# Batch 0 in whole products, batch 1's scores by subtiles, half of batch 2's second layer by seven products, and a new order

## The chip, the cores and the metric

The kernel runs on one core of a Trainium2 chip. Its engines are TensorE (PE in the rows; PEld its weight loads), VectorE (DVE), ScalarE (ACT), GpSimd (POOL) and SyncE (SP), which issues all transfers. The time is the device time of one execution, in microseconds, as the median of several runs. Each kernel also has one profiled execution, from which all rows are taken.

## What is computed

Local attention with block summaries, then a mixing of tokens of rank 32, then two dense layers over the channels, for 4 batches of 768 tokens, 8 heads of 64 channels and 512 channels in all:

```python
def _attn_ref(q, k, v):                      # (4, 8, 768, 64) each
    k_sum = k.reshape(B, H, nb, 32, D).max(axis=3)
    v_sum = v.reshape(B, H, nb, 32, D).mean(axis=3)
    scores = concat(where(|i - j| < 16, q @ k.T / 8, -1e9), q @ k_sum.T / 8 + log(32))
    return softmax(scores) @ concat(v, v_sum)

def _moe_ref(x, U, V, w_ch1, w_ch2):         # x: (4, 768, 512)
    h = x.transpose(0, 2, 1) @ U @ V         # over the tokens, rank 32
    u = x + h.transpose(0, 2, 1)
    return u + maximum(u @ w_ch1, 0) @ w_ch2 # 512 -> 2048 -> 512
```

U, V, w_ch1 and w_ch2 come as float64 and are turned into float32 on the chip.

## The kernel before

**Precision and products.** A dense product takes three products of a high and a low part each (high x high, high x low, low x high), every one a matrix product of TensorE in fp32r. A "part" is made by ScalarE, which rounds (`nc.scalar.copy(hi, ...)`), and by GpSimd or VectorE, which subtracts (`lo = whole - hi`). In the rows, `L1320` is the up layer (512 to 2048) of batches 1 to 3, `L1416` their down layer (2048 to 512), `L1522` batch 3's down layer, `L1024` and `L1049` are up and down of batch 0.

**Four batches, one after the other.** TensorE works on the dense layers of batch b, while the attention of batch b+1 is strewn in between: scores (`S`), exponentials (`E`, on VectorE and ScalarE), turning of the probabilities by VectorE and a way through HBM (`T`, `s`, `f`), values (`P`), normalising (`N`), the mixing (`M`, `J`, `O`). The attention of batch 0 has nothing beside it and fills the first 50 us.

**Batch 0** (L1300 on): for each of 16 slices f of the hidden layer and each half hf of the tokens (384), `up_channel` (L1015) makes 12 products of 384 columns over the four channel tiles, `up_out` takes the positive part as gates, and `down_rows` (L1043) takes three token tiles of the gates as the standing operand against 512 columns of w_ch2, 9 products. Its output has tokens on the rows. `leave_row` copies it out of PSUM, and `finish_rows` (L1063) turns it by 24 transposes (`ps_o`, L1068) within batch 1's up phase, adds u and stores it. Weights come by `load_weight` (L804) into five places for each layer, are turned to float32 (`t`), split, and, for the later batches, stored in HBM together with sums of them (`U`, `Us`, `D`).

**Batches 1 to 3, up** (`up_phase`, L1333): the matrices are cut in quarters, and seven products take the place of eight; a step is 6 products of 384 columns. **Down** (`down_phase`, L1396) in batches 1 and 2: whole products, channels on the rows; for each f four tiles of 512 columns and two of 2 x 256, 24 products, kept in six PSUM banks over all f. Batch 3 (`second_phase`, L1502) uses seven products for the down layer too: 56 steps of 6 products of 384 columns. Its operands are sums and differences of hidden quarters, made by `second_operand` (L1433) into places that `st.ring` hands out.

**Batch 1's scores** (`scores`, L436): a tile of 128 queries against 120 keys, with 128 rows of which half are zeros by `clear_gaps`, three tiles in a bank. Batches 0, 2 and 3 use `scores_by_subtiles` (L454): products of 64 x 64 in four corners of the array, 12 for a head, in two banks.

**Order.** `PLAN` is a text of words, cut by slashes. Each word writes one operation; at each step of TensorE's dense work `go()` (L1292) writes the words up to the next slash. A word with a dot ahead belongs to batch 0's attention. `F` loads a weight of a later batch, `p0` makes its high part and `p1` its low part. Each engine does its operations in the order in which they were written and waits only for data and places. `keep_busy` (L1147, `ps_w`) writes filler products that nothing reads.

```python
for f in range(NF):
    for hf in range(2):
        g = first.pop() if first else up_out(up(st, hf, f))
        go()
        if prev is not None:
            ...
            down_rows(accs[phf], pf, pg, pf == 0, pf == NF - 1)
            go()
        prev = (f, hf, g)
```

## Time and profile before

| | |
|---|---|
| median of 3 runs (lowest, highest) | 624.52 us (622.56, 624.90) |
| profiled execution | 623.3 us |
| its span in the trace | 621.5 us |
| TensorE, VectorE, ScalarE, GpSimd busy | 97%, 69%, 56%, 47% of the span |
| moved by transfers | 148.29 MB, 239 GB/s over the span |

The trace has a start and a duration for each operation. Neighbouring matrix products overlap in it, so that the duration of one (some 340 ns for 384 columns) is longer than its distance to the next. The chain of waits goes back from the last operation to what released it; in it, a piece's length is the time until the next piece. A matrix product on fp32 data has two records.

### The profile page before, as it was taken

The numbers are of one execution on the slowest core, as the hardware profiler recorded it, in microseconds if no ns is written. First come the engines' busy times: TensorE is split into PE (matmuls) and PEld (weight loads), VectorE is DVE, ScalarE is ACT, GpSimd is POOL, SyncE is SP. The second block draws the span as 40 slices with busy tenths as digits, with TensorE's granted clock in tenths as the row PEclk, the third lists the DMA queues.
The fourth block names the chain that finished last, engine by engine and source line by source line (L and its number), as shares of the span: only waits on it lengthen the run. The fifth ranks groups of instructions, "written<-read, shape, count | busy, mean of one in ns | idle before, by whom it ended". The sixth has DMA issues, their size and how long they took to land.

```text
span 621.5 us, 14548 instructions
## 1 busy us (share of the span) xinstructions
PE 605.7 (97%) x5336; PEld 550.0 (88%) x5336; DVE 427.1 (69%) x1141; ACT 349.6 (56%) x796; POOL 292.2 (47%) x360
## 2 busy tenths in 40 slices
PE   4899999999999999999999999999999999999997
PEld 2678989889888999998888899998888899999997
DVE  3778576767866877888788754665555652678994
ACT  1867575654563567665544556765452646675720
POOL 4451342534245868765443788663232676640000
PEclk9999999999999999999999999999999999999999
DMA  7997999999788788788889678778989653446443
GB/s 220 264 278 265 290 296 291 300 301 304 260 242 239 244 281 275 238 254 263 253 264 294 200 259 223 194 227 220 306 247 308 203 197 118 125 144 248 147 148 113
DMA packets 97702, 148.29 MB, mean 239 GB/s; under 512 B 9696, under 2 KB 68064, under 8 KB 97632
## 3 DMA queue, kind: packets, MB, share of 16 engines
q1 hardware_dynamic: 97632, 147.38, 77.2%
q8 instruction: 42, 0.69, 0.5%
q14 instruction: 28, 0.23, 0.1%
HBM read 104.67 MB, written 42.66 MB: 237 GB/s over the span
## 4 chain that ended last, share of the span: by engine, by line
PE 89%; DMA 5%; SPq 2%; ACT 1%; DVE 1%; issue 1%; POOL 0%; DVEq 0%
PE ps_h L1320 28%; PE acc L1416 19%; PE ps_h L1024 10%; PE acc L1049 10%; PE accx L1522 4%; PE ps_x L607 3%; PE accy L1522 3%; PE accz L1522 3%; PE ps_s L468 2%; PE ps_s L445 2%; DMA place<-rows 1%; DMA rows<-place 1%; DMA place<-in_v 1%; DMA place<-in_k 1%; PE ps_m L637 1%; PE ps_x L593 1%
## 5 line engine op out<-in xcount | busy, mean ns | idle before, releaser
L971 POOL TENSOR_TENSOR parts<-whole,parts 128x512 fp32r<-128x512 f32 (+1 forms) x128 | 160.5, 1269 | 96.8 <-ACT parts L967 84.3
L1320 PE MATMUL ps_h<-place,parts 128*128 128x384 f32 x1008 | 180.4, 336 | 0.0
L1320 PEld LDWEIGHTS ps_h<-place,parts 128*128 128x128 f32 x1008 | 174.4, 188 | 1.5 <-issue 0.5
L1416 PE MATMUL acc<-gh,parts 128*128 128x256 f32 (+1 forms) x512 | 134.2, 342 | 0.0
L1416 PEld LDWEIGHTS acc<-gh,parts 128*128 128x128 f32 x512 | 88.4, 189 | 12.1 <-issue 1.2
L967 ACT CAST parts<-whole 128x512 fp32r<-128x512 f32 (+1 forms) x144 | 80.1, 581 | 12.9 <-DMA whole<-down 4.0
L1416 PE MATMUL acc<-gl,parts 128*128 128x512 f32 (+1 forms) x256 | 86.5, 338 | 0.0
L278 POOL TENSOR_TENSOR place<-val,place 128x512 fp32r<-128x512 f32 x29 | 38.1, 1328 | 95.5 <-ACT place L277 63.0
L1024 PE MATMUL ps_h<-place 128*128 128x384 f32 x384 | 73.8, 340 | 0.5 <-DVE gl L1040 0.5
L1024 PEld LDWEIGHTS ps_h<-place 128*128 128x128 f32 x384 | 67.0, 188 | 3.2 <-DVE gl L1040 0.9
L503 ACT ACTIVATE e<-e,neg 128x120 f32<-128x120 f32 x144 | 51.6, 390 | 31.3 <-DVE neg L493 30.3
L1049 PE MATMUL acc<-place,gh 128*128 128x512 f32 x192 | 66.5, 400 | 0.0
L1389 ACT ACTIVATE gh<-place 128x768 fp32r<-128x768 f32 x32 | 26.9, 844 | 51.5 <-PE acc L1416 51.4
L1394 DVE SCALAR_TENSOR_TENSOR gl<-place,gh 128x768 fp32r<-128x768 f32 x32 | 36.1, 1129 | 25.4 <-ACT gh L1389 25.1
L1416 PEld LDWEIGHTS acc<-gl,parts 128*128 128x128 f32 x256 | 48.5, 189 | 4.3
L1049 PEld LDWEIGHTS acc<-place,gh 128*128 128x128 f32 x192 | 36.0, 188 | 7.6 <-ACT gh L1039 0.2
L747 POOL TENSOR_TENSOR place<-tmp,place 128x384 fp32r<-128x384 f32 x24 | 26.8, 1126 | 29.8 <-ACT place L743 29.8
L1039 ACT ACTIVATE gh<-ps_h 128x384 fp32r<-128x384 f32 x32 | 15.7, 490 | 43.5 <-PE ps_h L1024 43.4
L1040 DVE SCALAR_TENSOR_TENSOR gl<-ps_h,gh 128x384 fp32r<-128x384 f32 x32 | 17.8, 555 | 32.1 <-ACT gh L1039 32.1
L493 DVE CUSTOM_DVE_ANT_0 e<-ps_s,mask_sb 128x120 f32<-128x120 f32 x144 | 34.8, 275 | 6.0 <-PE ps_s L445 3.3
L1049 PE MATMUL acc<-place,gl 128*128 128x512 f32 x96 | 37.7, 393 | 0.0
L523 DVE STREAM_TRANSPOSE squares<-e 128x768 f32<-128x768 f32 x24 | 23.3, 971 | 16.6 <-ACT e L503 14.6
(152 smaller groups left out, 985.2 us busy)
## 6 DMA issues: line engine op xcount, KB each, us to landing
place<-in_w SPq DMA_DIRECT2D x32, 512.0 KB, 5.9
whole<-up SPq DMA_DIRECT2D x24, 512.0 KB, 4.9
there<-squares SPq DMA_DIRECT2D x24, 384.0 KB, 4.7
at<-there SPq DMA_DIRECT2D x96, 96.0 KB, 3.9
whole<-up SPq DMA_DIRECT2D x24, 384.0 KB, 4.5
whole<-down SPq DMA_DIRECT2D x16, 512.0 KB, 5.9
vt<-in_v SPq DMA_DIRECT2D x48, 146.2 KB, 4.4
kt<-in_k SPq DMA_DIRECT2D x24, 288.0 KB, 5.0
```

The lines of the kernel that those rows point to most:

```text
L278: engine.tensor_tensor(lo, val, f32(hi), ALU.subtract)
L493: nc.vector.tensor_tensor_reduce(out=e[:, u, :], in0=ps[:, i * KC : (i + 1) * KC], in1=mask_sb[:, m, :], scale=-SCALE, scalar=BIG, op0=ALU ...
L503: nc.scalar.activation(e[:, u, :], e[:, u, :], AF.Exp, bias=st.neg[h][:, u : u + 1], scale=-1.0,)
L967: nc.scalar.copy(hi, whole)
L971: (nc.vector if key[0] == "second" else nc.gpsimd).tensor_tensor(lo, whole, f32(hi), ALU.subtract)
L1024: nc.tensor.matmul(ps[:, :NH], w_split[0, f][:, c % 2, part_w, c // 2], ut[c], start=(c == 0 and n == 0), stop=(c == NC - 1 and n == 2),)
L1049: nc.tensor.matmul(acc[t], gt[:, sl], w_split[1, f][:, part_w], start=(first and j == 0), stop=(last and j == 2),)
L1320: nc.tensor.matmul(ps, a[:, sa, i], b[i][:, sb], start=(first and n == 0), stop=(n == 5), skip_group_check=not first,)
L1389: nc.scalar.activation(gh, h, AF.Relu)
L1394: nc.vector.scalar_tensor_tensor(gl, h, 0.0, f32(gh), ALU.max, ALU.subtract)
L1416: nc.tensor.matmul(place, w[:, part_w, c * P : (c + 1) * P], gt[:, q0:q1], start=(f == 0 and i == 0 and j == 0), stop=(f == NF - 1 and j = ...
L1522: nc.tensor.matmul(ps[:, part], w[j][:, sa, c * P : (c + 1) * P], gate[sb][:, part], start=fresh and q == 0 and j == 0 and k == 0, stop=(q ...
```

## The change

- **Batch 0, up:** no longer by `up_channel` and gates at once. `first_up_phase` keeps the 12 products of 384 columns per slice and half, in two half groups of 6 (channels 0 and 2, then 1 and 3); the first four groups do their first halves ahead, so that up can begin while channels 1 and 3 are still being mixed. The result goes to the hidden places, and gates come later, as in batches 1 and 2. The heads are taken in the order 0, 1, 4, 5, 2, 3, 6, 7.
- **Batch 0, down:** by channels, in the `down_phase` of batches 1 and 2; `leave_row`, `finish_rows` and its transposes go, and each output tile leaves at the end of its sum.
- **Batch 1's scores:** by `scores_by_subtiles`; `scores` and `clear_gaps` go.
- **Batch 2's down:** the first four of eight pairs of slices by seven products (28 steps of 6), the other four by whole products as before.
- **Weights of batch 0** come through the same three places as the later batches' (`load_place`), and are split by the same `p` words; a third word, `p2`, makes a low part on VectorE. Sums of weights may be made on GpSimd (`wp`).
- **PLAN** is written anew: 557 steps, 481 before, with 13 fillers ahead of the first up product, 6 before. Steps and order of batch 3's two phases stay.

```diff
-SEVEN = (3,)
+SEVEN = {2: 4, 3: 8}
+AHEAD = 4
+HEADS = (0, 1, 4, 5, 2, 3, 6, 7)
...
-    def weight_place(i, f, dt=F32):
-        return wt.tile([P, 2 * DM], dt, name="place", tag=f"w{i}_{f % RING}")
...
+    load_tags = ("w2", "w0_1", "w0_2")
...
+    def load_place(name, dt):
+        n_loads[0] += 1
+        return wt.tile([P, 2 * DM], dt, name=name, tag=load_tags[n_loads[0] % 3])
 
     def load_weight(i, f):
-        t = weight_place(i, f, I32)
+        t = words[i, f] = load_place("words", I32)
         nc.sync.dma_start(out=t, in_=(w1, w2)[i][:, f].bitcast(I32))
...
+    def first_up_phase(st):
+        live, weight = {}, {}
+        def half(f, hf, i):
+            if f not in weight:
+                weight[f] = use_weight("U", f)
+            if i == 0:
+                live[f, hf] = half_bank("ps_h")
+            ps = live[f, hf]
+            for n, c in enumerate((0, 2) if i == 0 else (1, 3)):
+                u = st.op[BLOCKS[hf, c % 2]][c // 2]
+                for k, (sa, sb) in enumerate(((0, 0), (0, 1), (1, 0))):
+                    nc.tensor.matmul(
+                        ps,
+                        weight[f][c % 2][:, sa, c // 2],
+                        u[:, sb],
+                        start=(i == 0 and n == 0 and k == 0),
+                        stop=(i == 1 and n == 1 and k == 2),
+                    )
+            if i == 1:
...
+                nc.scalar.copy(st.h[f // 2][f % 2][:, hf], live.pop((f, hf)))
+        groups = list(itertools.product(range(NF), range(2)))
+        first = [(*g, i) for i in range(2) for g in groups[:AHEAD]]
+        for step in first + [(*g, i) for g in groups[AHEAD:] for i in range(2)]:
+            half(*step)
+            yield
...
+        first, then = ("B11", "B21", "T1", "T2", "T3"), ("B22", "T4")
+        if st.b < B - 1:
+            first, then = ("T1", "T2", "B21", "T4"), ("B11", "T3", "B22")
+        once = len(places) + 2 * len(first)
...
             st.ring[m] = places[k][0]
-            free_at[k] = last
+            free_at[k] = 8 * NF if st.b < B - 1 and k < once else last
...
-        for i in range(8 * len(OPS)):
+        for i in range(2 * groups * len(OPS)):
...
+    def down_phases(st):
+        n = SEVEN.get(st.b, 0)
+        if n:
+            yield from second_phase(st)
+        if 2 * n < NF:
+            yield from down_phase(st, 2 * n)
...
-    for b in range(1, B):
+    for b in range(B):
         ends = []
-        for _ in up_phase(sts[b], ends):
+        for _ in up_phase(sts[b], ends) if b else first_up_phase(sts[0]):
             go()
-        if b in SEVEN:
-            phase = with_ends(ends, (1, 2), second_phase(sts[b]))
-        else:
-            phase = with_ends(ends, (1, 3), down_phase(sts[b]))
+        phase = with_ends(ends, {0: (), 1: (1, 3)}.get(b, (1, 2)), down_phases(sts[b]))
         for _ in phase:
             go()
```

The order of TensorE around the first up product of batch 0 (`ps_m`, `ps_r` and `ps_u` are the mixing, `ps_h` is up), before:

```order
L671 MATMUL ps_u<-ident_sb,x 128x128 x6
L637 MATMUL ps_m<-x,u_sb 32x128 x6
L655 MATMUL ps_r<-t_888,rep_sb 128x128
L681 MATMUL ps_u<-vm_st,t_st 128x384
L1151 MATMUL ps_w<-kt 128x512
L655 MATMUL ps_r<-t_904,rep_sb 128x128
L681 MATMUL ps_u<-vm_st,t_st 128x384 x2
L671 MATMUL ps_u<-ident_sb,x 128x128 x6
L681 MATMUL ps_u<-vm_st,t_st 128x384 x2
L1024 MATMUL ps_h<-place 128x384 x24
L1049 MATMUL acc_1020<-place,gh 128x512
```

And after:

```order
L643 MATMUL ps_u<-vm_st,t_st 128x384
L617 MATMUL ps_r<-t_951,rep_sb 128x128
L633 MATMUL ps_u<-ident_sb,x 128x128 x6
L643 MATMUL ps_u<-vm_st,t_st 128x384 x2
L599 MATMUL ps_m<-x,u_sb 32x128 x6
L1179 MATMUL ps_h<-place,parts 128x384 x6
L617 MATMUL ps_r<-t_993,rep_sb 128x128
L643 MATMUL ps_u<-vm_st,t_st 128x384
L633 MATMUL ps_u<-ident_sb,x 128x128 x3
L1179 MATMUL ps_h<-place,parts 128x384 x6
L643 MATMUL ps_u<-vm_st,t_st 128x384
L1179 MATMUL ps_h<-place,parts 128x384 x6
```

Up begins while mixing is still in the order, six products at a time, where it began with 24 behind all of the mixing; down no longer follows within batch 0's up.

TensorE again, where batch 2's down layer begins behind its up layer, before:

```order
L468 MATMUL ps_s<-kt,qz_85 64x120 x12
L607 MATMUL ps_x<-vt,at 32x65 x24
L1320 MATMUL ps_h<-place,parts 128x384 x6
L1416 MATMUL acc_6035<-gh,parts 128x512
L1416 MATMUL acc_6035<-gl,parts 128x512
L1416 MATMUL acc_6035<-gh,parts 128x512
L1416 MATMUL acc_6050<-gh,parts 128x512
L1416 MATMUL acc_6050<-gl,parts 128x512
L1416 MATMUL acc_6050<-gh,parts 128x512
L1320 MATMUL ps_h<-place,parts 128x384 x6
L1416 MATMUL acc_6063<-gh,parts 128x512
```

And after (`accx`, `accz` and `accy` are the sums of the seven products, `gate` their operands):

```order
L1153 MATMUL ps_h<-place,parts 128x384 x84
L569 MATMUL ps_x<-vt,at 32x65 x24
L1153 MATMUL ps_h<-place,parts 128x384 x12
L1395 MATMUL accx_6167<-gate,parts 128x384 x6
L1395 MATMUL accx_6177<-gate,parts 128x384 x6
L1153 MATMUL ps_h<-place,parts 128x384 x6
L438 MATMUL ps_s<-kt,qz_85 64x120 x12
L569 MATMUL ps_x<-vt,at 32x65 x24
L1395 MATMUL accx_6167<-gate,parts 128x384 x6
L1153 MATMUL ps_h<-place,parts 128x384 x6
L1395 MATMUL accx_6177<-gate,parts 128x384 x6
L1395 MATMUL accz_6321<-gate,parts 128x384 x6
```

Steps of 4 x 3 products of 512 and of 4 x 3 of 256 columns have become steps of 6 products of 384.

SP's order at the end of batch 0 (`rows<-place` sends turned rows of batch 1, `place<-rows` fetches them, `at<-there` fetches turned probabilities, `down<-val` stores a weight, `whole<-up` loads a weight for batch 1), before:

```order
L933 DMA whole<-up_104 128x1024
L552 DMA rows<-place 128x768
L536 DMA at<-there 32x4x192 x4
L299 DMA kt<-in_k 128x3x192 x2
L561 DMA place<-rows 32x4x192 x4
L894 DMA down<-val 128x512
L318 DMA qz_84<-in_q 64x384 x2
L552 DMA rows<-place 128x768
L354 DMA place<-in_vn 128x512 x2
L894 DMA down<-val 128x512 x2
L318 DMA qz_85<-in_q 64x384 x2
L561 DMA place<-rows 32x4x192 x4
```

And after, where `words<-in_w` is a load of a weight of batch 0:

```order
L800 DMA down<-val 128x512
L795 DMA up_110<-val 128x2x128
L754 DMA words<-in_w 128x1024
L800 DMA down<-val 128x512 x4
L506 DMA at<-there 32x4x192 x4
L754 DMA words<-in_w 128x1024
L303 DMA qz_84<-in_q 64x384 x2
L522 DMA rows<-place 128x768
L848 DMA whole<-up_104 128x1024
L800 DMA down<-val 128x512
L522 DMA rows<-place 128x768
L531 DMA place<-rows 32x4x192 x4
```

Two loads of weights of batch 0, 512 KB each, stand within the last issues ahead of the rows, where there were none.

## Rows read from the trace of the kernel before

**Rows 1.** The page's part 1: busy us, share of the span, instructions of each engine.

```profile
PE 605.7 (97%) x5336; PEld 550.0 (88%) x5336; DVE 427.1 (69%) x1141; ACT 349.6 (56%) x796; POOL 292.2 (47%) x360
```

**Rows 2.** Stages from:to; length, each engine's busy us, granted clock, DMA share, GB/s.

```profile
0.00:50.00 50.00, 39.34 (x711) 28.59 (x712) 31.98 (x162) 29.25 (x85) 22.30 (x62) 1.00 0.92 264
50.00:208.00 158.00, 157.48 (x1215) 140.57 (x1214) 111.87 (x300) 89.90 (x213) 60.12 (x73) 1.00 0.91 280
208.00:357.10 149.10, 148.34 (x1405) 133.86 (x1404) 118.47 (x298) 84.99 (x184) 94.09 (x111) 1.00 0.82 251
357.10:501.00 143.90, 143.55 (x1334) 130.11 (x1333) 83.09 (x235) 82.25 (x177) 78.19 (x84) 1.00 0.80 240
501.00:618.10 117.10, 117.04 (x679) 116.90 (x677) 81.07 (x151) 63.24 (x138) 37.50 (x32) 1.00 0.48 157
```

**Rows 3.** TensorE's waits, the longest: who <- whom, us in total, times, longest.

```profile
PE ps_s L468 <- POOL place L427: 6.1, 1, 6.1
```

**Rows 4.** The chain of waits in batch 0: start us, length us, what.

```profile
60.77 2.10 PE ps_h L1024 x12
62.87 0.66 PE ps_s L445 x6
63.53 2.09 PE acc L1049 x9
```

**Rows 5.** The chain of waits in batches 1 to 3.

```profile
236.65 0.81 PE ps_o L1068 x6
...
244.76 0.78 PE ps_s L468 x24
...
280.12 4.17 PE acc L1416 x24
...
290.26 4.38 PE acc L1416 x24
...
374.83 1.39 PE ps_s L468 x48
...
560.32 1.04 PE accx L1522 x6
```

**Rows 6.** Groups of instructions by shape: xcount, busy us, mean ns, idle before; last, DMA issues.

```profile
L747 POOL TENSOR_TENSOR place<-tmp,place 128x384 fp32r<-128x384 f32 x24 | 26.8, 1126 | 29.8 <-ACT place L743 29.8
L1460 DVE TENSOR_TENSOR gate<-place,gate 128x384 fp32r<-128x384 f32 x41 | 25.8, 651 | 3.0 <-ACT gate L1454 3.0
...
L262 DVE SCALAR_TENSOR_TENSOR val<-place,val 128x512 int32<-128x512 int32 x32 | 22.6, 725 | 0.1
...
L240 ACT ACTIVATE place<-place 128x512 f32<-128x512 f32 x32 | 21.0, 677 | 0.1
...
L1446 DVE TENSOR_TENSOR place<-place 128x384 f32<-128x384 f32 x8 | 4.4, 550 | 0.0
...
place<-in_w SPq DMA_DIRECT2D x32, 512.0 KB, 5.9
```

**Rows 7.** The chain of waits from the last value products to the first up product.

```profile
43.35 0.80 PE ps_u L671 x6
...
47.59 0.86 PE ps_w L1151 x2
...
49.02 0.66 PE ps_u L671 x6
49.67 0.35 PE ps_u L681 x2
50.03 1.21 PE ps_h L1024 x7
```

**Rows 8.** One stretch of the table; SP's issues, start us and length us.

```profile
70.00:100.00 30.00, 30.00 (x210) 27.20 (x209) 20.72 (x65) 18.16 (x48) 11.34 (x21) 1.00 0.99 297
...
166.10 0.43 SPq L806 DMA_DIRECT2D place<-in_w  x1
...
191.26 0.35 SPq L552 DMA_DIRECT2D rows<-place  x1
```

739 lines of the change are left out of this document (304 added, 435 removed).

## The prediction

> **What bounds the kernel now.** I read the engine totals first: TensorE is busy 605.7 of 621.5 us, VectorE 69% of the span [rows 1]. The table by stage [rows 2] says where the other 15.8 us lie. TensorE lacks 10.7 us in the first 50 us, and in the four stages after that 0.5, 0.8, 0.4 and 0.1 us; 3.4 us are the tail after its last product. Its granted clock is 1.00 in each stage, the upper of its two levels, 2.4 GHz. The list of its waits has one long one, 6.1 us ahead of the first score product [rows 3]. So from 50 us on the time is the sum of TensorE's instructions: what an edit takes from them is gained, unless it makes a wait. I price them in the chain of waits, by the distance from one start to the next, since busy times of neighbours overlap.
>
> **Prices.** In batch 0, 12 up products take 2.10 us, 9 down products of 512 columns 2.09 us, and the 6 records of three whole score products (each runs in two passes) 0.66 us [rows 4]. Later, 24 down products (half of 512, half of 256 columns) take 4.17 us, 6 products of 384 columns 1.04 us, 6 transposes 0.81 us, a head's scores by subtiles 0.78 us, two such heads in a row 1.39 us; and 24 down products right behind a head's scores take 4.38 instead of 4.17 us [rows 5]. So a single head by subtiles costs 0.78 + 0.21 = 0.99 us.
>
> **Batch 0's products.** The up phase keeps its 384 products of 384 columns: 32 x 2.10 = 67.2 us before, 64 half groups x 1.04 = 66.6 us after. Down takes 32 x 2.09 = 66.9 us by rows and 16 x 4.17 = 66.7 us by channels. I book **-0.5** us (0.8, rounded down) for both. What goes is the turning of the output: 24 transposes, 4 x 0.81 = **3.2 us**, all in batch 1's up phase, where TensorE has no gap that would hide them.
>
> **Batch 1's scores.** 16 banks x 0.66 = 10.6 us become 8 x 0.99 = 7.9 us: **-2.7**. The ends: all heads in pairs without an extra, 8 x 0.70 = 5.6 us, so -5.0; with 1.1 us a head, -1.8. I take the middle, since most heads stand alone in the new order. By the trace a record by subtiles costs 0.78/24 = 33 ns against 0.66/6 = 110 ns, 3.4 times less. The Trainium skill (TensorEngine Tiling (Array Packing), section Available Configurations) calls 64x64 four independent tiles; with a full factor of four a head would take 0.66 us and this term would be -5.3. The trace does not reach that, so its price stays.
>
> **Batch 2's down.** Half of 16 steps, 8 x 4.17 = 33.4 us, become 28 x 1.04 = 29.1 us: **-4.2** (before rounding 4.24). The operands of seven products must be made for that. VectorE gets, by the written order, 14 additions and 12 combinations of 550 ns and 12 low parts of 651 ns within this stretch, 22 us, beside the softmax, turning and normalising of three heads; GpSimd makes ten more low parts at 1126 ns [rows 6]. That fills VectorE nearly for the length of the stretch, 29.1 us of products and three heads' scores and values. The last operands are written one to three steps of 1.04 us ahead of their products, and six places take them in turn. In batch 3 the same kind of phase lies in a stage with 0.1 us of idle [rows 2], but it has more places. The ends are 0 and 4.2, the whole saving; I take **+1.0**, near batch 3's row.
>
> **The start.** TensorE waits 6.1 us for its first score product [rows 3]; from the last value product to the first up product, at 50.0 us, 6.7 us pass [rows 7]. In the new order the first four heads' scores are those of heads 0, 4, 1, 5, whose keys and queries lie behind 3.4 MB of transfers, where it was 2.7 MB: at the 264 GB/s of this stage 2.6 us later. Seven more filler products (ps_w, a pair of records 0.86 us) stand in the order; they cost nothing while TensorE waits anyway, 6 us if it doesn't. Against that, up may begin with channels 0 and 2 alone. Behind its start move two turns (0.66), three products of 384 columns (0.53) and a small one, 1.4 us in all; ahead of it move batch 1's first scores, 1.0 us. ScalarE and VectorE are busy 29 and 32 of these 50 us [rows 2]; ScalarE gets some 7 us more by the order, which still fits. I put the start of up at 51.0 us, with 46.5 and 55 as ends. With the 0.4 us of moved work this is **+1.4**, from -3.1 to +5.4.
>
> **Transfers in batch 0.** Here another resource is nearly full: the DMA engines' share is 0.99 at 297 GB/s from 70 to 100 us [rows 8] and 0.91 at 280 GB/s over the stage [rows 2]. What ends the stage is batch 1's turned rows: the last of them is sent off at 191.3 us [rows 8], and batch 1's up phase begins at 208.0, 16.7 us later. Up to that issue SP's transfers add up to 52.5 MB, in the new order to 53.4 MB, and the last two weights (512 KB each) stand 12 and 6 issues ahead of it, where no weight was loaded behind 166.1 us [rows 8]. With 264 x 50 = 13.2 MB in the first 50 us, 40.2 MB remain. At 280 GB/s they take 143.6 us, to 193.6, and batch 1's up could begin at 210.3. TensorE itself would be there at 51.0 + 154.7 = 205.7: the 157.5 us that it was busy in this stage, 0.5 less for the products, 3.7 less for scores (10.6 to 7 x 0.99), 1.4 more for the mixing left over. That is a lag of 4.6 us. At 297/0.99 = 300 GB/s, full engines, the rows leave at 184.0 and there is none. I take **+2.0**, between the two, since the written order leaves 14 to 15 us behind that issue, not 16.7.
>
> The full engines at 300 GB/s are the row's limit. The Trainium skill (DMA: Bandwidth & Descriptors, section Specifications) gives about 358 GB/s from HBM to one core; by that there would be no lag, and 615 us. The row speaks against it, as 297 GB/s already fill the engines. It would end within the forecast's own band, and I give it 0.06 of that band's chance.
>
> Weights now have three places to land in instead of ten. One round is a landing of 5.9 us, 0.68 us on ScalarE and two steps of at most 0.73 us on VectorE [rows 6], 8.0 us for three weights or 2.7 a weight; TensorE needs one in 4.2 us. So 4.5 us of queueing per load are free.
>
> **The sum.** 623.3 us, the profiled execution (621.5 of span and 1.8 around it), -3.2 -2.7 -4.2 -0.5 +1.4 +2.0 +1.0 = -6.2: 617.1, so **617 us**. The profiled execution lies 1.2 us below the median of the runs shown, 624.5; I don't correct for that.
>
> **Rivals.**
> 1. *A cheap start and no lag.* If the fillers all fall into idle time and half of the 6.7 us of mixing overlaps with products, the start gives -3.1 instead of +1.4; with the 3.0 us of booked waits gone, 617.1 - 4.5 - 3.0 = 610 us. For it: TensorE is idle 10.7 us there. Against: the later keys, and the transfer of the mixing weights (vm_st), which stands behind 10.6 MB.
> 2. *The gain is used up.* VectorE's full stretch in batch 2 gives the 4.2 us back as waits (3.2 over the 1.0 booked), and the lag is 4.6 (2.6 over): 617.1 + 5.8 = 623 us. For it: the late operands. Against: VectorE is busy only 83 of 144 us in that batch [rows 2].
> 3. *Transfers drag batch 0, slower than before.* ScalarE's conversion stands at the head of its queue until a weight has landed; the copies of up products stand behind it, the next load behind the conversion, and the DMA engines go idle in between. If 280 GB/s falls to 260, 40.2 MB take 154.6 us, the rows leave at 204.6 and batch 1's up begins at 221.3, 15.6 us late: 617.1 + 13.6 = 631 us. It decides from 265 GB/s: 151.7 us, 218.4, a lag of 12.7, and 627.8 us. Against: 280 GB/s was reached with SP's own waits among it.
> 4. *It does not do what it says.* If subtiles brought nothing in batch 1, 619.8 us, within the forecast's band.
>
> **How the numbers follow.** Forecast with its band, 612 to 621.4: 0.58, rival 4 and the page's 615 among it. Rival 1, 605 to 612: 0.20. Rival 2, 621.4 to 627.6: 0.14. Rival 3: 0.08. The likeliest is 617 us. The range of 607 to 624 holds the forecast's band, most of rival 1 and more than half of rival 2, 0.82 together. 0.5%, about what a measurement of this kernel can tell from no change, is 3.1 us around 624.5, so the borders are 621.4 and 627.6: faster 0.78, same 0.14, slower 0.08.
>
> **What would show it.** In the changed profile: no transposes of output rows; a head of batch 1's scores near 0.8 us; 28 steps of 1.04 us in batch 2; the first up product near 51 us; a DMA share above 0.93 from 50 to 205 us; a gap of about 2 us around the start of batch 1's up phase and of about 1 us within batch 2's seven products. The prediction is wrong if gaps of over 5 us lie inside batch 0, if the first up product comes after 55 or before 46 us, or if six products of 384 columns cost other than 1.04 us.

## The result: slower by 1.3%, where 1.2% faster was forecast

| | before | after |
|---|---|---|
| median (lowest, highest) | 624.71 us (622.56, 625.13) | 632.11 us (631.01, 634.09) |
| ratio of after to before, 95% interval | | 1.0129 [1.0094, 1.0164] |
| profiled execution, its span | 623.3, 621.5 us | 632.54, 630.8 us |

The new kernel is 7.4 us slower by the medians; 617 us, within 607 to 624, was forecast. One execution of r7 (643.53 us) and one of r9 (1188.15 us) were in a slow state and are left out of their medians below. Part 1 of after's page, beside [rows 1]:

```profile
PE 610.0 (97%) x5508; PEld 550.3 (87%) x5508; DVE 476.2 (76%) x1182; ACT 360.3 (57%) x821; POOL 277.5 (44%) x375
```

TensorE is busy 4.3 us longer, not shorter: some 8 us longer in the start and 3.8 less behind it. VectorE has 49 us more to do. The table by stage of after, beside [rows 2]: from:to, length, busy us of TensorE, its weight loads, VectorE, ScalarE and GpSimd, granted clock, DMA share, GB/s. The stages are the start, batch 0, and batches 1 to 3, each to the first up product of the next.

```profile
0.00:57.00 57.00, 47.22 (x752) 30.86 (x752) 34.56 (x169) 33.56 (x94) 19.41 (x55) 0.97 0.86 232
57.00:213.70 156.70, 155.70 (x1417) 140.27 (x1416) 121.98 (x292) 93.34 (x207) 75.00 (x100) 1.00 0.90 282
213.70:365.60 151.90, 147.91 (x1359) 132.23 (x1358) 117.93 (x288) 80.78 (x178) 75.76 (x103) 0.99 0.80 244
365.60:507.90 142.30, 141.32 (x1310) 129.92 (x1309) 114.40 (x278) 88.72 (x206) 79.78 (x96) 1.00 0.80 250
507.90:627.10 119.20, 117.81 (x680) 116.98 (x678) 86.75 (x159) 63.85 (x139) 27.50 (x24) 1.00 0.49 161
```

With before's stages cut at the same products (start 49.9, then 157.9, 149.2, 143.9 and 117.2 us) the misses are:

| stage | change forecast | change measured |
|---|---|---|
| start, to the first up product | +1.0 | +7.1 |
| batch 0 (scores, products, moved work; lag +2.0) | -0.8 | -1.2 |
| batch 1 (transposes) | -3.2 | +2.7 |
| batch 2 (sevens -4.2, waits +1.0) | -3.2 | -1.6 |
| batch 3 | 0 | +2.0 |
| sum | -6.2 | +9.0 |

One head's scores of batch 2 (0.8 us) stand in batch 0 in after and in batch 1 in before; like with like, batch 0 is at -2.0 and batch 1 at +3.5.

**The prices of the pieces hold, their sum does not.** The chain of waits of after: start, length, what, beside [rows 5].

```profile
145.84 4.37 PE acc L1281 x24
150.21 0.78 PE ps_s L438 x24
...
434.03 1.24 PE accx L1395 x6
...
436.31 1.04 PE accx L1395 x6
437.35 4.16 PE accz L1395 x24
```

A head of batch 1's scores takes 0.78 us, six products of batch 2's sevens 1.04. So the single prices were right. Batches 1 to 3 together were forecast at -6.4 us and came at +3.1: TensorE's idle time there rose by 5.2 us (1.0 booked), a spell of half clock cost 1.7 (nothing booked), and the rest of their time, without the moved head, fell by 3.0 where 7.4 were booked. What the other 4.4 are is not shown. They may be short waits: six products of 384 columns take 1.04 us, 0.17 each, but are recorded with some 0.34, so a wait of up to 0.17 us does not show as idle time. The waits that do show in after (who waits <- for whom, us in total, times, longest), where [rows 3] had one long wait and nothing over 0.8 us behind 50 us:

```profile
PE ps_s L438 <- POOL place L414: 2.6, 1, 2.6
PE ps_x L555 <- ACT place L545: 1.9, 1, 1.9
PE ps_s L438 <- issue: 1.6, 1, 1.6
PE ps_t L539 <- issue: 1.5, 1, 1.5
PE ps_h L1153 <- DVE parts L898: 1.4, 2, 1.2
PE ps_h L1153 <- ACT place L1232: 1.4, 2, 1.1
...
PE ps_n L380 <- issue: 1.0, 1, 1.0
```

**The waits behind batch 0 come mostly from VectorE.** The longest stands at 309 us. The timeline of after there (start, length, engine, line, what; in brackets idle time before and for whom):

```profile
306.39 2.27 DVE L414 COPY kt<-km 64x48 f32<-64x48 f32 x4
...
307.34 1.27 POOL L898 TENSOR_TENSOR parts<-whole,parts 128x512 fp32r<-128x512 f32 x1
...
309.10 0.56 DVE L585 TENSOR_TENSOR x<-ps_x,sum 128x384 f32<-128x384 f32 x1
...
307.75 0.42 PE L438 MATMUL ps_s<-kt,qz 64*64 64x120 f32 x2
309.76 0.84 PE L438 MATMUL ps_s<-kt,qz 64*64 64x120 f32 x22 [1.59 <-issue]
```

The wait is put down to "issue", but it ends 0.1 us behind the end of the division L585 (309.66), which empties the PSUM bank that the second bank of these scores takes. It stood behind four small copies, which took 2.27 us beside a GpSimd low part and 0.75 us alone. What follows the gap, in the same columns as the stages:

```profile
308.00:310.00 2.00, 0.41 (x11) 0.28 (x13) 1.92 (x6) 0.70 (x1) 0.61 (x1) 1.00 1.00 295
310.50:314.00 3.50, 3.50 (x11) 2.80 (x9) 3.46 (x13) 1.69 (x4) 0.77 (x1) 0.51 0.69 144
314.00:315.00 1.00, 1.00 (x6) 0.81 (x6) 1.00 (x1) 0.00 (x0) 1.00 (x2) 1.00 1.01 407
```

For 3.5 us the granted clock is the lower level, 1.2 GHz: another 1.7 us lost, so that a wait of 1.6 us costs 3.3 in this execution. The same wait of 1.59 us stands in r1, r2, r3, r6, r7 and r8 below too; a spell follows it in r3 and r8, and none in the other four. The other wait of over a microsecond in batch 1:

```profile
258.33 2.30 DVE L898 TENSOR_TENSOR parts<-whole,parts 128x512 fp32r<-128x512 f32 x1
...
258.54 1.27 POOL L898 TENSOR_TENSOR parts<-whole,parts 128x512 fp32r<-128x512 f32 x1
259.77 0.31 POOL L360 TENSOR_TENSOR vsum<-vsum,stage 128x64 f32<-128x64 f32 x1
```

A low part of 128x512 takes VectorE 0.68 us when GpSimd does nothing (median of 44); beside a working GpSimd the median is 0.77 (of 28), nine take over 1.0, and this one 2.30. The up products that read it wait 1.20 us, to 260.69. VectorE makes 82 low parts of weights now, 66 more than before. The Trainium skill (SBUF — State Buffer, section SBUF: two separate sides) says that VectorE and GpSimd have one pair of ports in common, which one of them holds for a whole instruction, also against a VectorE instruction with two inputs in SBUF. The size agrees: 1.62 us are added beside 1.27 + 0.31 us of GpSimd. Who waits does not show: VectorE's record began first and was still the longer one.

In batch 3, whose products and their order are as before, the wait comes through a chain:

```profile
514.35 0.70 DVE parts L898
515.05 0.02 SPq L848
...
515.10 4.61 DMA whole<-up
...
520.26 0.38 ACT place L1232
...
520.68 3.39 PE ps_h L1153 x18
```

Once a low part for batch 3's up layer is ready, at 515.05, SP loads the next weights, which land at 519.7. ScalarE's queue stands for weights that land then, and behind that stands its copy `L1232`, which reads the PSUM bank that the next up product writes. That product starts at 520.68, after 1.10 us of waiting.

**The start.** TensorE's timeline in after:

```profile
12.62 1.65 PE L438 MATMUL ps_s<-place,x 64*64 64x120 f32 x24 [2.55 <-POOL place L414]
14.20 2.08 PE L1009 MATMUL ps_w<-kt 128*128 128x512 f32 x2
...
17.34 1.98 PE L1009 MATMUL ps_w<-kt 128*128 128x512 f32 x4
...
25.91 0.38 PE L539 MATMUL ps_t<-ident_sb,gl 128*120 128x128 f32 x2 [1.46 <-issue]
...
34.86 0.57 PE L555 MATMUL ps_x<-place 120*64 120x65 f32 x12 [1.93 <-ACT place L545]
...
41.00 0.78 PE L380 MATMUL ps_n<-place,means_w 120*32 120x65 f32 x39 [1.03 <-issue]
...
56.99 1.33 PE L1179 MATMUL ps_h<-place,parts 128*128 128x384 f32 x6
```

Before had one gap of 6.1 us, done by 9.5 us, and behind it none over 1.1. After has four of 1.0 to 2.6 us, and its fillers (26 records ps_w, 12 before) stand between them: 16.1 us of TensorE by the distance of starts, 7.5 before. In all, TensorE's idle time in the start is 9.8 us, 10.7 before, so it is not idle longer. Leaving the fillers out, TensorE was busy for 5.6 us by 20 us before and 4.4 after, 17.2 and 10.7 by 35 us. The last scores of batch 0 come at 37.3 us instead of 34. From there to the first up product, in before and in after (columns as in the stages):

```profile
34.00:49.90 15.90, 15.85 (x290) 12.72 (x288) 11.71 (x45) 11.65 (x33) 9.49 (x19) 1.00 1.00 316
```

```profile
37.30:57.00 19.70, 18.27 (x382) 14.77 (x380) 16.74 (x67) 14.09 (x40) 6.57 (x13) 1.00 0.61 169
```

TensorE is busy in nearly all of it. So of the 7.1 us, 3.3 are later last scores, 2.4 are more work of TensorE's own that the new order leaves behind them (92 records more, mostly values and batch 1's first scores), and 1.4 are waits. Between 40 and 50 us the DMA engines are busy for 0.32 of the time, so by then the transfers do not look like what it waits for.

### The profile page after: what moved, and what is told of

Its sections match the earlier page's. It is cut to its first block, busy times and chain, and to the rows that moved or that the text cites. A ratio compares the mean times of both kernels' runs of the same rounds, so it can differ in the third digit from the quotient of the medians.

```text
span 630.8 us, 14980 instructions
## 1 busy us (share of the span) xinstructions
PE 610.0 (97%) x5508; PEld 550.3 (87%) x5508; DVE 476.2 (76%) x1182; ACT 360.3 (57%) x821; POOL 277.5 (44%) x375
## 4 chain that ended last, share of the span: by engine, by line
PE 73%; DMA 9%; DVE 8%; ACT 3%; issue 3%; SPq 2%; POOL 2%; DVEq 0%; POOLq 0%; ACTq 0%
PE ps_h L1153 22%; PE acc L1281 17%; PE ps_h L1179 10%; PE accx L1395 5%; PE accz L1395 4%; PE accy L1395 3%; PE ps_s L438 3%; DMA kt<-in_k 3%; PE ps_x L569 2%; DVE parts L898 2%; DMA place<-rows 2%; DMA there<-squares 1%; PE ps_w L1009 1%; PE ps_x L555 1%; DMA at<-there 1%
## 5 line engine op out<-in xcount | busy, mean ns | idle before, releaser
L1153 PE MATMUL ps_h<-place,parts 128*128 128x384 f32 x1008 | 181.3, 337 | 2.8 <-DVE parts L898 1.4
L1153 PEld LDWEIGHTS ps_h<-place,parts 128*128 128x128 f32 x1008 | 174.0, 188 | 6.6 <-DVE parts L898 2.1
L1281 PE MATMUL acc<-gh,parts 128*128 128x512 f32 (+1 forms) x640 | 169.3, 344 | 0.8 <-DVE x L1418 0.8
L898 POOL TENSOR_TENSOR parts<-whole,parts 128x512 fp32r<-128x512 f32 (+1 forms) x85 | 107.9, 1281 | 82.7 <-ACT parts L893 66.6
L1281 PEld LDWEIGHTS acc<-gh,parts 128*128 128x128 f32 x640 | 111.5, 190 | 16.9 <-issue 2.7
L1179 PE MATMUL ps_h<-place,parts 128*128 128x384 f32 x384 | 69.7, 337 | 0.3 <-DVE place L681 0.3
L1179 PEld LDWEIGHTS ps_h<-place,parts 128*128 128x128 f32 x384 | 66.3, 188 | 1.8 <-issue 0.8
L898 DVE TENSOR_TENSOR parts<-whole,parts 128x512 fp32r<-128x512 f32 (+1 forms) x65 | 50.9, 791 | 4.4 <-ACT parts L893 4.2
L1319 ACT CAST gate<-place 128x384 fp32r<-128x384 f32 x65 | 31.4, 511 | 23.0 <-DVE place L1311 8.3
L1395 PE MATMUL accx<-gate,parts 128*128 128x384 f32 x204 | 38.6, 337 | 0.1
L1395 PEld LDWEIGHTS accx<-gate,parts 128*128 128x128 f32 x204 | 35.5, 188 | 0.9 <-DVE parts L898 0.4
L1325 DVE TENSOR_TENSOR gate<-place,gate 128x384 fp32r<-128x384 f32 x52 | 33.4, 659 | 3.5 <-ACT gate L1319 3.4
```

The source lines that it names most:

```text
L898: (nc.vector if last else engine).tensor_tensor(lo, whole, f32(hi), ALU.subtract)
L1153: nc.tensor.matmul(ps, a[:, sa, i], b[i][:, sb], start=(first and n == 0), stop=(n == 5), skip_group_check=not first,)
L1179: nc.tensor.matmul(ps, weight[f][c % 2][:, sa, c // 2], u[:, sb], start=(i == 0 and n == 0 and k == 0), stop=(i == 1 and n == 1 and k == 2),)
L1281: nc.tensor.matmul(place, w[:, part_w, c * P : (c + 1) * P], gt[:, q0:q1], start=(f == f0 and i == 0 and j == 0), stop=(f == NF - 1 and j ...
L1319: nc.scalar.copy(hi, val)
L1325: engine.tensor_tensor(lo, val, f32(hi), ALU.subtract)
```

## The experiments

All stages in us, from each kernel's profiled execution; the ratio is against the kernel before on the same chip. Lines in these kernels mostly stand one ahead of those of after (L437 for L438). Batches 2 and 3 have the same order in after, r1, r6, r7 and r8 and take 141.3 to 143.5 and 118.0 to 119.2 us there, so a difference of a microsecond in one stage of one execution tells nothing.

| run | start | b0 | b1 | b2 | b3 | median | ratio, 95% |
|---|---|---|---|---|---|---|---|
| before | 49.9 | 157.9 | 149.2 | 143.9 | 117.2 | 624.71 | |
| after | 57.0 | 156.7 | 151.9 | 142.3 | 119.2 | 632.11 | 1.013 [1.009, 1.016] |
| r1_few_fillers | 56.8 | 156.1 | 152.6 | 143.5 | 118.0 | 631.33 | 1.012 [1.007, 1.017] |
| r2_gp_lows | 57.8 | 163.8 | 152.6 | 145.1 | 117.7 | 641.53 | 1.028 [1.026, 1.030] |
| r3_b2_whole | 57.6 | 156.1 | 156.4 | 144.9 | 117.2 | 635.6 | 1.018 [1.015, 1.022] |
| r4_b1_subtiles | 50.5 | 163.7 | 148.5 | 144.2 | 117.2 | 629.82 | 1.011 [1.008, 1.014] |
| r5_norm_early | 59.4 | 156.8 | 151.1 | 146.4 | 119.2 | 634.01 | 1.017 [1.012, 1.022] |
| r6_start_gp | 57.6 | 157.2 | 151.8 | 141.3 | 118.6 | 632.73 | 1.013 [1.008, 1.018] |
| r7_more_fillers | 55.7 | 157.9 | 159.3 | 141.8 | 118.8 | 633.5 | 1.018 [1.012, 1.023] |
| r8_b1_whole | 57.1 | 158.2 | 153.4 | 142.9 | 118.1 | 635.5 | 1.017 [1.013, 1.022] |
| r9_fixes | 57.9 | 156.8 | 150.1 | 141.4 | 118.5 | 629.35 | 1.009 [1.006, 1.012] |
| r10_start_loads | 56.4 | 157.0 | 154.1 | 140.9 | 118.8 | 630.47 | 1.009 [1.006, 1.012] |
| r11_start_keys | 61.0 | 156.0 | 151.2 | 143.2 | 117.2 | 633.09 | 1.014 [1.010, 1.018] |
| r12_start_built | 58.1 | 156.8 | 151.0 | 142.1 | 117.2 | 633.26 | 1.017 [1.014, 1.021] |
| r13_gaps_filled | 58.8 | 158.2 | 151.9 | 142.9 | 117.2 | 630.94 | 1.013 [1.010, 1.017] |
| r14_gaps_filled_few | 55.6 | 156.5 | 152.9 | 141.5 | 118.6 | 631.01 | 1.013 [1.011, 1.015] |
| r15_scores_early | 58.9 | 156.3 | 149.3 | 141.7 | 119.0 | 631.33 | 1.012 [1.009, 1.015] |
| r16_scores_early_two | 58.8 | 156.5 | 150.2 | 139.9 | 118.9 | 630.62 | 1.011 [1.009, 1.013] |
| r17_no_block | 56.5 | 156.0 | 150.9 | 142.0 | 118.8 | 626.7 | 1.004 [1.002, 1.007] |
| r18_before_bare | 51.1 | 158.0 | 152.1 | 144.4 | 117.2 | 625.41 | 1.001 [0.999, 1.003] |

### Parts of the change, one by one

**r1_few_fillers.** Eight of after's 13 filler words go, as at this place:

```diff
-.E10.1 .E2.1 .w1 .M0 .C0
+.E10.1 .E2.1 .M0 .C0
```

> The changed kernel with 8 of its 13 filler steps (16 of 26 records of ps_w) taken out, all behind the first two heads' scores; nothing else is touched. Theory A: the fillers stand in TensorE's way. From 17.3 us on they take 7.7 us by the distance of starts, and TensorE has only 4.4 us of idle time between them and the first up product; so that product comes at 50 to 52 us where it was 57.0, and the time falls by 5 to 7 us, to 625 to 627. Theory B: the start is set by the later keys and by ScalarE's queue; the fillers only fill idle time, the first up product stays at 56 to 57 us and the time at 631 to 632. Theory C: without them TensorE's granted clock falls to 0.5 in the gaps, and the time rises by 1 to 3 us.

The first up product comes at 56.8 us, 0.2 earlier, though 7.5 us of fillers are gone. The wait at 33 us grew to 2.8 us, and the spells of half clock in the start from 13.5-17.0 us to 13.5-17.5, 20.5-28 and 34-38 us, 5.1 us more lost. So the eight fillers alone do not cause the late start: without them longer gaps (1.5 us more in all) and a lower clock behind them take their room.

**r2_gp_lows.** All 66 low parts that VectorE makes go to GpSimd:

```diff
-.L1.2 p2 c0.3
+.L1.2 p1 c0.3
```

> The changed kernel with all 66 low parts that its order gives to VectorE (0.68 us alone, up to 2.3 us beside GpSimd) on GpSimd, as nearly all were before. Theory A: VectorE's low parts make the late operands in batches 1 to 3 (waits of 1.2, 0.8, 0.8 and 0.2 us for VectorE behind 208 us); they go, and the time falls by 2 to 4 us, to 628 to 630. Theory B: VectorE is not the cause, but weights that land late; GpSimd at 1.1 us for each gets 73 us more and is late in its turn, 633 to 638 us.

Slower still by 9 us, 7 of them in batch 0 (its row; columns as in the stages):

```profile
57.80:221.60 163.80, 158.75 (x1417) 142.00 (x1416) 121.93 (x275) 91.48 (x202) 96.58 (x116) 0.99 0.87 269
```

GpSimd has 97 us to do instead of 75, at 1.3 us a part (median of that stage). TensorE is idle for 5.0 us in batch 0, 1.0 in after, the longest wait being 2.5 us for turned probabilities with a spell of half clock behind it. So in this order the work cannot simply be moved back.

**r3_b2_whole.** After up to ten steps ahead of batch 2's up layer, then before's order, without sevens in batch 2. VectorE's low parts in batches 2 and 3, 30 of the 66, go back to GpSimd with it, so the run does not part the two:

```diff
-SEVEN = {2: 4, 3: 8}
+SEVEN = {3: 8}
```

> The changed kernel's order up to ten steps ahead of batch 2's up phase, and from there the order before: batch 2's down with whole products only, low parts on GpSimd. Batch 0 and batch 1 stay as changed. Theory A: the gain of the seven products in batch 2 (4.2 us forecast) is used up by waits: batches 2 and 3 took 265.1 us in the changed kernel and 264.3 us before, so the time is 631 us, within 1 us of the changed kernel. Theory B: the seven products gain what was forecast and the loss lies elsewhere: 634 to 636 us.

The total alone would mislead: 3.5 us slower than after, but 4.1 us more lie in batch 1's down layer, where the order is the same and two spells of half clock fell, one in after. Batch 2's down layer, in r3 and in after:

```profile
433.90:515.00 81.10, 80.38 (x746) 68.80 (x745) 48.61 (x115) 41.50 (x85) 32.83 (x29) 1.00 0.83 251
```

```profile
429.10:507.90 78.80, 77.82 (x746) 69.45 (x745) 71.32 (x154) 44.79 (x99) 35.70 (x33) 1.00 0.82 256
```

Sevens and VectorE's low parts together bring 2.3 us there, with VectorE at 71 instead of 49 us. But batch 3's up layer takes 56.2 us in r3, as before, and 58.1 in after: 1.9 us go back, net 0.4 us. Batch 3's nine low parts are only part of that: r9, where GpSimd makes them, still takes 57.5. In the runs with after's order there it is 57.0 to 58.2 us, so the size of the net is not settled, only that it is far below 4.2.

**r4_b1_subtiles.** Before, with batch 1's scores by subtiles, each head at one place (head 0 of batch 1 has half of its queries zero, with the same amount of work):

```diff
-S1.0.1 ... S1.0.0
+S1.0
...
-return [3 * a + i if st.b == 1 else 2 * i + a for i in range(3)]
+return [2 * i + a for i in range(3)]
```

> The kernel before with one edit: batch 1's scores by subtiles, all six tiles of a head at the place of its second bank's scores; batch 0, batch 2 and batch 3 stay. Theory A, the term of the forecast: 16 banks at 0.66 us become 8 heads at 0.99 us, 2.7 us less, 621 to 622 us, or down to 619.5 if the heads cost no extra. Theory B: a head takes two banks at once and its exponentials come later in VectorE's queue, which makes waits: 624 to 626 us.

Batch 0 takes 163.7 us, 5.8 more, with TensorE busy 1.7 less; eight waits of 0.8 to 0.9 us stand in it, 7.0 together, like this one:

```profile
79.53 0.84 PE L461 MATMUL ps_s<-kt,qz 64*64 64x120 f32 x22 [0.89 <-DVE gl L1033]
```

A head by subtiles takes two PSUM banks at once, and all banks come from one supply. Here its products wait until VectorE (`gl`) has read an up product's bank; in five of the eight it is the next up products, behind the scores, that wait until VectorE (`neg`) or ScalarE (`e`) has come to these scores. The edit alone loses; it needs the new order around it.

**r8_b1_whole.** The counterpart: after, with whole score products in batch 1:

```diff
+if st.b == 1:
+    for u in range(NU):
...
+        nc.tensor.matmul(
+            ps[u // 3][:, (u % 3) * KC : (u % 3 + 1) * KC],
+            qt[:, 64 + j * P : 64 + j * P + P], kt[:, k0 : k0 + KC],
```

> The changed kernel with batch 1's scores as whole products again, six of a head at the one place where its scores by subtiles stand; nothing else in the order, but GpSimd clears the gaps of two query tiles first. Theory A, the term of the forecast: 16 banks at 0.66 us instead of 8 heads at 0.99 us, 2.7 us more, 634 to 635. Theory B: the saving is used up by waits, as TensorE is not what bounds there: 631 to 633.

3.4 us slower than after by the medians, with intervals that overlap, and 2.8 by the profiled spans; 1.5 of it lie in batch 0 and 1.5 in batch 1. In batch 0, where the scores are, TensorE is busy 2.6 us more (158.3 instead of 155.7) and idle 1.0 less. So in the new order the subtiles spare TensorE about the 2.7 us that were booked, and the stage about 1.5.

### The waits of batches 1 to 3

**r5_norm_early.** The division that emptied the bank late goes ahead of the turning and the copies:

```diff
+Kd2.7 N2.4 T2.6
...
-Kd2.7
...
-N2.4
```

> The changed kernel with three of VectorE's steps in batch 1's down in another order: the gap columns of batch 2's last head (2.27 us beside GpSimd) and the division of head 4's values (1.0 us) ahead of the turning of head 6's squares (0.97 us) instead of behind it; nothing else. Theory A: TensorE's wait of 1.59 us within that head's scores, shown as for nothing, is for the division: the scores take two banks at once and the second is the one whose values are still to be divided; it starts again 0.07 us after the division's end in each run so far. The wait goes, and with it the 3.3 us at half clock behind it (1.65 us lost): 3.2 us less, about 629. Theory B: the wait is the fetch of instructions or the keys' transfer and stays at 1.59 us: 632.

The wait at 309 us and its half clock are gone: batch 1's down layer takes 84.9 us, 87.2 in after. The cause of that wait is shown: it stands in after and in r1, r2, r3, r6, r7 and r8, and in none of the runs that have this move (r5, r9 to r17). The total does not show it: in this run a wait of 2.2 us came at 42 us and one of 2.3 us for a low part at 438 us, each followed by a spell of half clock.

**r9_fixes.** r5's move, an operand made earlier, and the last nine low parts given to GpSimd:

```diff
+Kd2.7 N2.4 T2.6
...
+y1.3 K2.7
...
-p2
+p1
```

> The changed kernel with three small moves, none in the start: the division of head 4's values and the gap columns of the last head ahead of the turning in batch 1's down, as before; there too one low part of gates (y1.3) ahead of the maxima of a key tile that lands late; and the last 9 low parts of weights that VectorE makes, all for batch 3's up, on GpSimd. Theory A: the late work in batches 1 and 3 is VectorE's, piece by piece: batch 1's down (87.2 us in the changed kernel) takes 83 us, batch 3's up (58.1) takes 56.5, the time falls by 5 to 6 us, to 626 to 627. Theory B: VectorE and the transfers are late as a whole, and a wait taken away comes back some steps later: stages within 1 us of the changed kernel's, 630 to 632.

2.8 us better than after by the medians, with intervals that overlap: batch 1 150.1 us, batch 3 118.5. The start is still 57.9.

### The start

**r6_start_gp.** Five small steps of the first heads go from ScalarE to GpSimd:

```diff
-.Ba0 a1.1.0 .Ba4 ... .Ka3 ... .Da4 ... .Da1
+.Bp0 a1.1.0 .Bp4 ... .Kp3 ... .Dp4 ... .Dp1
```

> The changed kernel with five steps of its start (four copies of value sums and one head's four gap copies, 3.1 us) on GpSimd instead of ScalarE; nothing else. Theory A: ScalarE's queue sets the start: TensorE's wait of 1.93 us for ScalarE's copy at 34.9 us goes, what stands behind comes 2 to 3 us earlier, the first up product at 54 to 55 us where it was 57.0, the time at 629 to 630. Theory B: keys and their gap columns set it, and TensorE's order: the first up product stays at 56 to 57.5 us, the time at 631 to 633.

The wait at 34 us fell to 0.72 us, but the first up product came at 57.6. That wait was not the one that decides.

**r7_more_fillers.** Three more fillers in the gap at 10 us:

```diff
-.E1.0 .w1 .S4
+.E1.0 .w1 .w1 .w1 .w1 .S4
```

> The changed kernel with three filler steps more (2.6 us), in the gap of 2.55 us ahead of the second head's scores; nothing else. Theory A: that gap is why TensorE's granted clock is 0.5 from 14 to 17.4 us; filled, the clock stays at 1.00, scores and fillers there take 1.7 us less, and the first up product comes at 55.3 us, the time at 630 to 631. Theory B: the start does not hang on TensorE's pace there: first up product at 57 us, 632.

The spell at 14 to 17 us is gone and the start is 1.3 us shorter. Others came, of which only the first stands near the edit: 33-36.5, 244.5-248.5 and 302.5-310 us, and batch 1 took 159.3 us.

**r10_start_loads.** r9, with the first weight's load and early sums moved back:

```diff
-.E11.2 W0.0 .E10.1
+.E11.2 .E10.1
...
-.lr .lv1
+.lr .lv1 W0.0 l1.1.0
```

> The kernel with the three moves of r9, and in the start 1.0 MB of transfers (batch 1's first value sums and the first weight) behind the last values of batch 0 instead of ahead of them; the two additions that use them move behind too. Theory A: the transfers' order sets the start: values, keys and fetched instructions land up to 4 us earlier, TensorE's waits at 24 to 26 us and 40 to 41 us shrink, the first up product comes at 53 to 55 us where it was 57.0. Theory B: the start is set by the scores' order and TensorE's pace ahead of 35 us; first up product at 56 to 58 us.

Start 56.4 us; its "issue" waits are gone. VectorE now stands 2.5 us for that weight (32.8 us).

**r11_start_keys.** r10, with the keys and queries of heads 0, 4 and 1 loaded first:

```diff
-.w1 .lk0 .K0 .Kd0 .lu .lk2 .lm .li .K2 .lq0 .lk5
+.w1 .lk0 .K0 .Kd0 .lq0 .lk4 .lm .lq4 .lk1 .lu .lq1
```

> The kernel of r10, and in the start the keys and queries of heads 0, 4 and 1 as the first transfers, their maxima first in VectorE's queue, head 4's gap columns on VectorE, one filler step less. Theory A: head 4's scores come at 9.5 to 10.5 us instead of 12.6, no gap of over 1.5 us is left behind the first scores, TensorE's granted clock stays at 1.00, and the first up product comes at 51 to 53 us. Theory B: the gap only moves behind, to head 1's or head 5's scores, with a stretch at half clock again: 55 to 57 us.

Start 61.0 us: VectorE stood 7.2 us for the small table that now came later, and head 4's scores waited 6.4 us. The gap only moved.

**r12_start_built.** Against r11 the tables come ahead again, as here; r6's copies are in too, the means' weights come later, and 11 fillers are left:

```diff
-.lm .lq4 .lk1 .lu .lq1 .li
+.lm .lq4 .li .lk1 .lu .lq1
```

> The kernel of r10 with the copies of r6, and a start in another order: keys of heads 0, 4 and 1 first as in r11, but the means' weights, which wait for the identity's transfer, behind the first exponentials in VectorE's queue; 11 fillers. Theory A (gaps and the half clock behind them are the start's loss): head 4's scores come at 8 to 10 us, no gap over 1.5 us follows, no half clock behind 12 us, first up product at 50 to 52 us, the time at 623 to 625. Theory B (the start is bound elsewhere, by landings or ScalarE): first up product at 55 to 57 us, 628 to 630.

Start 58.1 us, with a wait of 4.7 us at 34 us, again behind the first weight's landing, for which VectorE stood 3.7 us.

**r13_gaps_filled, r14_gaps_filled_few.** r6 and r10 together, with fillers in the gaps: 18 in r13, 12 in r14.

```diff
+.w1 .w1 .w1 .S4
...
+.w1 .w1 .V3
```

> The kernel of r10 with the copies of r6, and five filler steps more: three ahead of the second head's scores, two ahead of the values that wait for ScalarE, 18 in all. Theory A: the clock stays at 1.00 all through the start, and the first up product comes 2 to 3 us earlier than in r10 (56.4): 53.5 to 54.5 us, although there are more fillers. Theory B: the clock does not matter there, the fillers add to TensorE's work: 57 to 59 us.

> r13 without the six filler steps that stand where TensorE has other work (5.3 us), 12 in all. Theory A: what is left in TensorE's way goes, and the clock stays: 51 to 52 us for the first up product, 624 to 626 for the time. Theory B: TensorE falls idle where the fillers stood, and runs at half clock behind it, as without fillers in r1: 55 to 57 us.

r13 had nearly the full clock (0.997) and the latest start of this pair, 58.8 us; r14 55.6 us with a spell at 22-29.5 us. What fillers save in clock they cost in time. So half clock alone is not what makes the start long.

**r15_scores_early, r16_scores_early_two.** r14, with the scores of heads 2, 6, 3 and 7 earlier in the order, or of 2 and 6 alone:

```diff
+.E8.0 .S2
+.E2.1 .S6
...
+.T8 .S3
+.V3 .S7
```

> The kernel of r14 with the scores of the last four heads earlier in TensorE's order: head 2's ahead of the first turned scores, head 6's ahead of the first means, heads 3's and 7's two to five steps earlier. Theory A: the late scores set the start, since VectorE and ScalarE wait for them: the last scores come at 31 to 33 us instead of 36 to 37, the first up product at 51 to 53 us (r14: 55.6), the time at 626 to 628. Theory B: the keys and queries of these heads land too late for the earlier places, TensorE waits there instead: 55 to 58 us.

> As r15, but the scores of heads 3 and 7 stay at their places; only those of heads 2 and 6 are earlier. Theory A: half of the gain of r15, first up product at 53 to 54.5 us. Theory B: no gain, 55 to 57 us.

Starts 58.9 and 58.8 us: in r15 the earlier scores wait 2.0 us for their queries' transfer. In both, VectorE stands for the first weight (`words<-in_w`), 1.9 us in r15 and 3.0 in r16, to 31.7 and 31.9 us, and TensorE waits 2.8 and 2.9 us, to 32.6 and 32.8.

**r17_no_block.** r15, with the first weight's conversion (`c0.0`, `t0.0`) behind the steps that it held up, and two fillers fewer:

```diff
-.V1 c0.0 t0.0 .E12.1
+.V1 .E12.1
...
+.E7.1 c0.0 t0.0
...
+.E13.2 t0.0
```

> r15 with the three steps that turn the first weight (one on ScalarE, two on VectorE) behind the first values of the second half, so that neither queue stands for that weight, and without the two filler steps ahead of the values that waited. Theory A: the scores' order and the wait for the weight held the start; both gone, the last scores come at 31 to 33 us, the first up product at 51 to 54 us, the time at 626 to 628. Theory B: the keys and queries of the later heads land too late for any earlier place, and what is behind them takes its 19 to 20 us: first up product at 55 to 58 us.

626.7 us, 5.4 better than after and the best of this order, 3.0 above the 623.68 of before on the same chip. The executions spread from 623.3 to 630.4; the profiled one took 629.6. Its longest waits in the start, in the columns of the waits above:

```profile
PE ps_s L437 <- DMA x<-in_q: 2.3, 2, 2.1
...
PE ps_n L379 <- issue: 1.6, 1, 1.6
```

The last scores come at 34.3 us, as in before, and yet the first up product at 56.5. In between:

```profile
34.30:56.50 22.20, 19.56 (x385) 16.29 (x381) 18.90 (x75) 16.18 (x44) 8.78 (x16) 0.92 0.74 214
```

TensorE is busy for 19.6 us there, 15.9 in before: 95 records more, and 1.7 us of a spell at 40-44. Another spell, at 23-27, cost 1.7 ahead of that. So the order of what stands behind the last scores, which none of these edits changed, keeps this start long by some 2 us.

### The clock by itself

**r18_before_bare.** Before, without its five later filler words, as at this place:

```diff
-.E11.1 .w1 .E10.0
+.E11.1 .E10.0
```

> The kernel before without the five filler steps behind its first one (10 records of ps_w, 5.4 us by the distance of starts); nothing else. Theory A: the fillers keep the gaps short; without them gaps of over 1.5 us open, TensorE's granted clock falls to 0.5 behind them, and the first up product comes at 50 to 53 us (before: 50.0), the time at 624 to 627. Theory B: the fillers only cost TensorE's time and the clock stays: first up product at 47 to 49 us, the time at 621 to 623.

A gap, and the stretches around what follows it:

```profile
19.16 0.47 PE L391 MATMUL ps_n<-place,means_w 96*32 96x65 f32 x16 [2.15 <-DMA place<-in_v]
```

```profile
16.00:21.00 5.00, 1.91 (x66) 1.40 (x69) 3.00 (x26) 3.47 (x12) 0.00 (x0) 1.00 1.04 230
21.00:28.00 7.00, 6.77 (x95) 5.32 (x86) 4.42 (x25) 4.72 (x16) 4.75 (x14) 0.51 0.91 258
28.00:33.00 5.00, 5.00 (x146) 4.38 (x143) 3.40 (x22) 3.85 (x13) 1.59 (x6) 1.00 0.74 230
```

The old order, which showed no half clock behind its first 13 us, gets it too once its gap is not covered: clock 0.51 for 7 us, and the start 1.2 us longer although 5.4 us of fillers are gone. A second gap of 2.1 us at 317 us, behind a transfer, brought a spell at 318-321.5 us. Over ten executions the median did not move: 1.0014 [0.9994, 1.0033].

## Why the prediction was wrong, step by step

- **Prices of single pieces, right.** Scores by subtiles 0.78 us a head, six products 1.04, down by channels 4.37 behind values (4.38 booked behind scores). No output transposes are left. By r8 the subtiles spare TensorE 2.6 us in batch 0, 2.7 booked.
- **"From 50 us on the time is the sum of TensorE's instructions": the step that failed.** The prediction took 0.1 to 0.8 us of idle in each stage of before to mean that what TensorE is spared is gained, and did not ask how far ahead of their products the operands were ready. In batches 1 to 3 TensorE's idle time went from 1.2 to 6.4 us, 1.0 being booked there, a spell of half clock took 1.7, and the rest fell by 3.0 instead of 7.4. VectorE's load was costed for batch 2 alone; the 66 low parts more, which lie in every batch, were not counted, nor was the price beside a busy GpSimd (up to 2.30 us for a part that takes 0.68 alone). For the wait at 309 us r5 shows VectorE's lateness as the cause; for the others the traces name the engine that ended them.
- **A wait was booked at its own length.** The one of 1.6 us cost 3.3 in after with the half clock behind it (the two stretches at 308 to 314 us; r18 shows the same behind a gap of 2.15 us). No term or rival had that. A spell there is not certain, though: in one execution each, four of the seven kernels with that wait had none.
- **Batch 2's sevens, mis-sized.** -4.2 by price. TensorE's work in the down layer fell by 2.5, with one more head's scores (0.8) in it; six products cost up to 1.24 us next to other work. The booked 1.0 us of waits within the seven products was 0.1; another 0.8 stands behind them, at 472 us, in the whole products. Batch 3's up layer, booked at 0, took 1.9 more than in r3.
- **The start, the largest miss: +7.1 for +1.0.** It lay outside the ends given (46.5 to 55). The keys' later transfer was seen (2.6 us), but "they cost nothing while TensorE waits anyway" (the fillers) failed: the fillers took 8.6 us more, and the idle time shrank by 0.9 only, since the gap came in four pieces with fillers between them. The forecast booked 0.4 us less of TensorE's work ahead of the first up product; behind the last scores there are 2.4 more. That a step at the head of ScalarE's or VectorE's queue holds everything behind it until a weight has landed was booked for batch 0 (rival 3) and occurs in the start (r10, r12, r15, r16; r17 takes it away, with two fillers, and is 4.6 us faster than r15). No run of this order brought its first up product ahead of 55.6 us. Why the last scores come 3.3 us later, and the tail's 1.4 us of waits, stay open.
- **Lag of the transfers, +2.0: not seen, and not settled.** The last rows leave at 196.5 us (193.6 computed), and batch 1's up layer begins at 213.7 without a gap. But batch 0 began 6 us later than booked, and that may have covered the lag. The DMA share that was named as a sign, above 0.93, was 0.91 from 57 to 205 us. Nor is 300 GB/s what full engines move in general: before's last 15.9 us ahead of its first up product show 316 at a share of 1.00.
- **Rival 3** has the right time (631) and the wrong mechanism: from 57 to 214 us the transfers run at 282 GB/s and a share of 0.90, as in before. **Rival 2** named the direction, VectorE's work giving the gain back, but in batch 2 alone; against it stood "VectorE is busy only 83 of 144 us". An average over a stage does not tell whether one part comes in time.

## What to carry to other kernels

A bound engine with no idle time says what an edit can gain at most. What it will gain depends also on whether the operands are finished in time. No run here measured how far ahead they were; before a change, take that distance from the trace for each stream of operands, and cost every operation moved to a helper engine at its price beside the other helpers, not alone. A gap of the bound engine can cost more than its length, when its clock falls behind it, and does not always. For a start, count what the order leaves to the bound engine behind the last operand that it has to wait for. And where single spells move by some us from one execution to the next, the stage of the edit shows its effect and the total may hide it (r3, r5).
